# Attention and two MLPs on one core: one weight conversion less in the head's middle, and two groups of first products kept open there instead of three

## The chip, the cores and the metric

One of the eight cores of a Trainium2 chip runs the whole program. The metric is the device time of one execution in microseconds (us). The engines are PE (TensorE, matrix products), DVE (VectorE), ACT (ScalarE), POOL (GpSimd) and SP (SyncE, which only issues DMAs here; ACT issues some as well). Each engine works through its own instructions in the order of the program and meets the others only at semaphores.

## The reference, cut to what matters

```python
scores = scale * q @ k.T + min(bias, 0), causal          # 2 batches x 8 heads, 576 tokens, head size 64
x = softmax(scores) @ v                                  # 1152 tokens x 512
h = x @ w_in ; y = max(0.01 * h, h) @ w_out              # first MLP, 2048 hidden
out = sum_e p_e * (max(y @ w1[e], 0) @ w2[e])            # 4 experts, 1024 hidden, p_e from domain_probs
```

`w_in` and `w_out` come as 64-bit numbers and are converted on the chip to 32-bit ones, sixteen pieces of 128x1024.

## The kernel before, in words

Nearly every instruction is issued through a wrapper at line 43 that keeps program order on its engine, so the order on each engine is the order in which the Python code below calls it, and all rows name L43.

**Attention.** The work is cut into 16 units (a batch, a pair of heads, and either the first 256 or the last 320 tokens). A unit of the first kind has 4 items, one of the second kind 6. `attention()` walks over the items: step `i` issues the scores of item `i`, the exponentials of item `i-1`, the transposes of item `i-3`, the products with the values of item `i-5` and the finish of item `i-7`, and it yields three times a step, so that other work can be put in between. Scores go to `ps_sc`, DVE writes them with their row minimum to `z`, ACT takes the exponential, PE transposes to `ps_pt`, ACT copies to `pv`, PE multiplies with the values into `ps_o` (one buffer), DVE divides into `xo`, PE transposes that to `ps_x`, ACT and DVE write `x0` as a rounded part and a remainder.

**The weights.** `supply()` converts one piece in six calls: ACT takes the absolute value of the upper words into `raw`; then two `TENSOR_SCALAR` and two `SCALAR_TENSOR_TENSOR` on DVE, 128x1024 each; then `finished`, which is called after the next piece's ACT operation: it stores `raw` to DRAM (`w_f`), fetches a further 1 MB piece, and, where a buffer is free and no reload is under way, calls `split_w`:

```python
nc.scalar.copy(w[:, 0], raw)                                              # rounded part, on ACT
nc.gpsimd.tensor_tensor(w[:, 1], raw, f32(w[:, 0]), ALU.subtract)         # remainder, on POOL
```

Pieces that are not split at once are reloaded later from `w_f` by `late_splits()`. There are three `raw` buffers for conversions and reloads together. For the second kind of units POOL also forms the remainders `qs` and `ks`.

**The first products.** `opening()` computes the first 128-row tiles of `x @ w_in` while attention still runs: for each of four slices `kk` (one pair of heads) it adds three products of 512 columns to each open group `ps_u`, which is a PSUM bank of `ps_mm` (three banks in this phase, one of them first used by `nothing`). The second of the three products reads the remainder of the weights.

**The head** is the loop up to step 38, in which units 0 to 7 end. At the transposes of a step it puts products of zeros on PE (`idling(n)`, `n` products 128x128 into `nothing`, without use for the result) or one step of `opening`; at a step's end it calls `supply()` once in some steps. **The weave** is the second loop, steps 39 to 86: with the other 8 units it runs 82 steps of the first MLP and twice a step one call of `late_splits()` and `supply()`. Then the rest of the first MLP follows with nothing of attention beside it, then the second half of its tokens and the experts.

Of the kernel before, what the change touches and what calls it, by code (L numbers as in the profile page):

```python
# [9 lines left out]
F32 = mybir.dt.float32  # L10
# [9 lines left out]
def attention_moe_moe2(ctx: ExitStack, tc: tile.TileContext, q, k, v, s, w_in, w_out, probs, w1, w2, out):  # L20
# [34 lines left out]
    P = 128  # L55
    KD = DM // P
# [55 lines left out]
    def fetch64(n):  # L112
        src, (rows, _) = stream[n][:2]
        r64 = r64p.tile([P, 1024, 2], U32, tag="r64", name="r64")
        r64s.append(r64)
        nc.scalar.dma_start(r64.rearrange("p (a b) t -> p a (b t)", a=rows), src)
# [122 lines left out]
    def in_order(blocks):  # L239


        for i in range(len(blocks) + 1):
            if i < len(blocks):
                yield "up", blocks[i], 0
            if i > 0:
                yield "down", blocks[i - 1], None
            if i < len(blocks):
                yield "up", blocks[i], 1
# [5 lines left out]
    def fetch(n):  # L254

        if fixed:
            return
        for i in range(len(ready), min(n, len(stream))):
            if i not in raws:
                raws[i] = load_w(*stream[i][:3])  # L260
        for i in range(len(ready), min(n, len(stream))):
            ready.append(split_w(raws.pop(i), stream[i][1], stream[i][4]))
# [3 lines left out]
    def next_w(k):  # L266

        nonlocal used, retired
        retired = used
        used += k  # L270
        fetch(used + look)
        return ready[used - k : used]
# [7 lines left out]
    def in_steps(ps, pairs):  # L280

        for i, ((wh, wl), (xh, xl)) in enumerate(pairs):
            for j, (a, b) in enumerate(((wh, xh), (wl, xh), (wh, xl))):
                nc.tensor.matmul(ps, a, b, start=(i == j == 0), stop=(i == len(pairs) - 1 and j == 2))
            if i < len(pairs) - 1:
                yield

    def at(x, *where):
        return x[(slice(None), 0) + where], x[(slice(None), 1) + where]

    x_t, y_t, oacc, touched = [], {}, {}, {}
# [4 lines left out]
    def evict_up(ps, h):  # L296
        ht = hpool.tile([P, 2, sizes[0]], F32R, tag="h", name="ht")
        h.append(ht)
        hi, lo = at(ht)
        nc.scalar.activation(hi, ps, AF.Prelu, alpha=0.01)  # L300
        nc.scalar.activation(ps, ps, AF.Prelu, alpha=0.01)
        nc.vector.tensor_tensor(lo, ps, f32(hi), ALU.subtract)

    def up1(w, h, tiles=(0, 1)):

        for i in tiles:
            sl = slice(i * P, (i + 1) * P)
            ps = ps_mm.tile([P, 512], F32, tag="mm", name="ps_u")
            yield from in_steps(ps, [(at(w, kk, sl), at(x_t[0], kk)) for kk in range(KD)])
            evict_up(ps, h)  # L310
            yield

    def opening(h):

        w = next_w(2)
        ps = [ps_mm.tile([P, 512], F32, tag="mm", name="ps_u") for _ in range(3)]
        for kk in range(KD):
            for i in range(3):
                wi, sl = w[i // 2], slice(i % 2 * P, (i % 2 + 1) * P)
                for j, (l, m) in enumerate(((0, 0), (1, 0), (0, 1))):  # L320
                    nc.tensor.matmul(ps[i], wi[:, l, kk, sl], x_t[0][:, m, kk], start=(kk == j == 0), stop=(kk == KD - 1 and j == 2))
                if kk == KD - 1:
                    evict_up(ps[i], h)
                yield
        yield from up1(w[1], h, (1,))

    def down1(f, c, h, w):

        if f == 0:
            y_t[c] = ypool.tile([P, KD, sizes[c]], F32, tag=f"y{c}", name=f"y{c}")  # L330
        for d in (0, 2, 1, 3):
            for lo, hi in halves(c):
                ps = ps_mm.tile([P, 512], F32, tag="mm", name="ps_d")[:, : hi - lo]
                sl, cols = slice(d * P, (d + 1) * P), slice(lo, hi)
                at_h = [at(x, cols) for x in h] if c == 0 else [at(x, j, cols) for x in h for j in range(2)]
                yield from in_steps(ps, [(at(w[i // 2], i % 2, sl), x) for i, x in enumerate(at_h)])
                ya = y_t[c][:, d, cols]
                if f == 0:
                    nc.scalar.copy(ya, ps)
                else:  # L340
                    nc.vector.tensor_tensor(ya, ps, ya, ALU.add)
                yield
# [111 lines left out]
    def mlps(blocks):  # L454
        hs = {}
        for what, (e, f, c), pair in in_order(blocks):
            h = hs.setdefault(f, [])
            if what == "down":
                yield from down1(f, c, h, next_w(2))
            elif c == 0 and f == 0:  # L460
                if pair == 0:
                    yield from opening(h)
            elif c == 0:
                yield from up1(next_w(1)[0], h)
            else:
                h.append(paired_up(next_w(1)[0], c, True))
                yield
# [20 lines left out]
    ps_mm = banks.enter_context(tc.tile_pool(name="ps_mm", bufs=3, space=PSUM))  # L488
# [39 lines left out]
    def idling(n):  # L528

        for _ in range(n):  # L530
            nc.tensor.matmul(nothing[:, :P], idle, idle, start=True, stop=True)
# [174 lines left out]
    done = 0  # L706
# [33 lines left out]
    def hidden_pool(stack, n):  # L740
        nonlocal hpool
        hpool = stack.enter_context(tc.tile_pool(name="hpool", bufs=n))
# [5 lines left out]
    with ExitStack() as phase:  # L748
        x_t[0] = phase.enter_context(tc.tile_pool(name="x0pool", bufs=1)).tile([P, 2, KD, sizes[0]], F32R, name="x0")
        wpool = phase.enter_context(tc.tile_pool(name="wpool", bufs=4))  # L750
        r64p = phase.enter_context(tc.tile_pool(name="r64p", bufs=2))
        side, units_of_w, late, opened = attention(), supply(), late_splits(), 0
        nothing = ps_mm.tile([P, 512], F32, tag="mm", name="nothing")
        with tc.tile_pool(name="early", bufs=1) as early:
            ones = pads(early)
            cumulative()
            main = mlps(phases[0])

            for at_ in range(3 * 64):
                i = next(side)  # L760
                if done == 2 * NP:
                    break
                if at_ % 3 == 0 and i in (6, 8):
                    nc.scalar.copy(q_s[i // 2 - 3][D:DK, 1], ones[D:DK])
                if at_ % 3 == 1:
                    if i < 20:
                        idling(2)
                    elif i >= 22 and opened < 3 * (done // 2) and (opened < 6 or i >= 30):
                        next(main)
                        opened += 1  # L770
                if at_ % 3 == 2:
                    if i in (1, 5):
                        fetch64(i // 4)
                    if i >= 8 and (i < 21 or i >= 29):
                        next(units_of_w)
        hidden_pool(phase, 6)

        owed = 0
        for at_, i in enumerate(side):
            if at_ % 3 < 2:  # L780
                owed += WOVEN * KD / (2.0 * (48 - 6))
                while owed >= 1.0:
                    next(main)
                    owed -= 1.0
            if at_ % 3 != 1:
                next(late, None)
                next(units_of_w, None)
        attn.close()
        w7pool = ctx.enter_context(tc.tile_pool(name="w7pool", bufs=2, side="right"))
        scratch = ctx.enter_context(tc.tile_pool(name="scratch", bufs=2, side="right"))  # L790
        t7pool = ctx.enter_context(tc.tile_pool(name="t7pool", bufs=1, side="right"))
        tokens = paired_steps(1, x_t[1], t7pool)
        banks.close()
        ps_mm = ctx.enter_context(tc.tile_pool(name="ps_all", bufs=8, space=PSUM))

        sevens = first_sevens()
        for m, _ in enumerate(main):
            if m % 2 == 0:
                next(late, None)
            if m % 4 == 0:  # L800
                next(tokens, None)
            if m % 4 == 2:
                next(units_of_w, None)
            if m % 4 % 2 and m >= 4:
                next(sevens, None)
        for _ in sevens:
            pass
        for _ in tokens:
            pass
# [57 lines left out]
```

## Time and profile before

| | |
|---|---|
| time, median of 3 runs | 748.9 us (747.37 to 749.19) |
| the profiled execution's own time | 745.92 us |
| its span, first to last instruction | 744.1 us |
| busy: PE, DVE, ACT, POOL | 97%, 57%, 44%, 44% |
| mean granted clock of PE | 0.989 of full speed |
| chain that ended last, by engine | PE 83%, DVE 6%, ACT 4%, DMA 2%, issue 2%, POOL 1% |

A busy share is an average over stages with different limits, and pipelined matrix products make a PE that has little to do look busy. So the stages are read one by one, and in each the waits of PE.

### The profile page before, as it was taken

Reading aid. Unit: us, or ns where it says so; the run is one execution under the profiler, and the core shown is the slowest. Engines: PE = TensorE matmul, PEld = TensorE weight load, DVE = VectorE, ACT = ScalarE, POOL = GpSimd, SP = SyncE. Lnnn points to the kernel's source line nnn. Section 1 sums busy time; section 2 is a strip of 40 time slices with the busy share of each in tenths; the row PEclk is TensorE's granted clock in tenths of the full one; section 3 lists DMA queues with packets and bytes.
Section 4 is the critical chain, followed back from the end, with each engine's and each line's share of the span. In section 5 each row is a group of like instructions: output and inputs, shape, how many; then the busy total and the mean of one; then the engine's idle time right before and its main releaser. Section 6 shows DMA issues by size and latency. Waiting matters only on the chain.

```text
span 744.1 us, 11402 instructions
## 1 busy us (share of the span) xinstructions
PE 718.6 (97%) x4388; PEld 652.7 (88%) x4388; DVE 424.4 (57%) x850; ACT 330.7 (44%) x643; POOL 324.0 (44%) x250
## 2 busy tenths in 40 slices
PE   9998889999999999999999999999999999999997
PEld 8887668788887899999988988989889898898996
DVE  4856787589825755853784444644445444454452
ACT  5668676677663666553351232312313223142220
POOL 4134354343236978895255271542705427053200
PEclk9999899999999999999999999999999999999999
DMA  6785666865431223221021210201102012020002
GB/s 162 221 215 161 194 166 199 268 205 195 151 109 62 58 92 107 85 86 58 29 78 36 57 57 1 86 29 57 56 1 86 29 57 58 0 80 7 1 29 99
DMA packets 40890, 69.39 MB, mean 93 GB/s; under 512 B 4004, under 2 KB 22980, under 8 KB 40836
## 3 DMA queue, kind: packets, MB, share of 16 engines
q1 hardware_dynamic: 32132, 43.50, 20.0%
q10 hardware_dynamic: 8704, 25.17, 10.0%
q8 instruction: 34, 0.56, 0.3%
q14 instruction: 20, 0.16, 0.1%
HBM read 57.83 MB, written 10.82 MB: 92 GB/s over the span
## 4 chain that ended last, share of the span: by engine, by line
PE 83%; DVE 6%; ACT 4%; DMA 2%; issue 2%; POOL 1%; ACTq 0%; SPq 0%; DVEq 0%; POOLq 0%
PE ps_d L43 40%; PE ps_u L43 33%; PE ps_o L43 5%; DVE raw L43 3%; PE ps_sc L43 3%; PE ps_pt L43 2%; DMA qr<-in_q_dram 1%; DMA r<-in_moe_w_in_dram 1%; DVE z L43 1%; PE nothing L43 1%; ACT z L43 1%; DVE t L43 1%; ACT w L43 1%; ACT pv L43 1%; ACT ps_u L43 0%
## 5 line engine op out<-in xcount | busy, mean ns | idle before, releaser
L43 POOL TENSOR_TENSOR w<-raw,w 128x1024 fp32r<-128x1024 f32 (+2 forms) x88 | 148.3, 1700 | 316.3 <-ACT w L43 303.1
L43 PE MATMUL ps_u<-t,w 128*128 128x320 f32 (+1 forms) x1680 | 237.3, 299 | 2.2 <-DVE t L43 1.2
L43 PEld LDWEIGHTS ps_u<-t,w 128*128 128x128 f32 x1680 | 233.2, 189 | 6.3 <-ACT w L43 1.5
L43 PE MATMUL ps_d<-w,ht 128*128 128x512 f32 x864 | 203.3, 391 | 0.0
L43 PEld LDWEIGHTS ps_d<-w,ht 128*128 128x128 f32 x864 | 160.2, 188 | 31.9
L43 ACT ACTIVATE ht<-ps_u 128x320 fp32r<-128x320 f32 (+2 forms) x176 | 74.4, 433 | 162.1 <-DVE ps_u L43 132.3
L43 PE MATMUL ps_d<-ht,w 128*128 128x320 f32 (+1 forms) x576 | 110.8, 342 | 0.9 <-DVE y L43 0.9
L43 DVE SCALAR_TENSOR_TENSOR oacc<-ps_d,pn,oacc 128x512 f32<-128x512 f32 x63 | 47.3, 751 | 104.3 <-PE ps_d L43 104.3
L43 ACT CAST w<-raw 128x1024 fp32r<-128x1024 f32 (+2 forms) x88 | 64.0, 757 | 83.6 <-PE ps_d L43 70.5
L43 PEld LDWEIGHTS ps_d<-ht,w 128*128 128x128 f32 x576 | 91.5, 189 | 6.8 <-ACT t L43 1.3
L43 PEld LDWEIGHTS ps_o<-vs,pv 128*128 128x128 f32 x480 | 65.6, 197 | 15.2 <-issue 8.8
L43 PE MATMUL ps_o<-vs,pv 128*128 128x65 f32 x480 | 65.0, 273 | 8.3 <-issue 5.4
L43 DVE TENSOR_TENSOR ps_u<-ps_u,tmp 128x320 f32<-128x320 f32 (+1 forms) x120 | 56.4, 471 | 27.5 <-PE ps_u L43 26.1
L43 DVE SCALAR_TENSOR_TENSOR ht<-ps_u,ht 128x320 fp32r<-128x320 f32 (+1 forms) x128 | 56.3, 452 | 23.3 <-ACT ht L43 22.0
L43 POOL TENSOR_TENSOR w<-sums,w 128x1024 fp32r<-128x1024 f32 x24 | 58.7, 2444 | 6.1 <-ACT w L43 6.1
L43 DVE TENSOR_TENSOR tmp<-ps_u,tmp 128x320 f32<-128x320 f32 (+1 forms) x80 | 37.0, 464 | 42.2 <-PE ps_u L43 40.2
L43 PE MATMUL ps_u<-x,w 128*128 128x512 f32 x192 | 58.7, 422 | 0.0
L43 DVE CUSTOM_DVE_ANT_0 z<-ps_sc,mask 128x256 f32<-128x256 f32 (+4 forms) x80 | 40.8, 512 | 29.3 <-PE ps_sc L43 22.6
L43 ACT ACTIVATE z<-z,mn 128x256 f32<-128x256 f32 (+4 forms) x80 | 48.6, 607 | 13.2 <-DVE mn L43 11.3
L43 ACT COPY pv<-ps_pt 128x512 f32<-128x512 f32 (+3 forms) x96 | 38.8, 422 | 26.8 <-PE ps_pt L43 24.1
L43 PE MATMUL ps_pt<-ident,z 128*128 128x128 f32 x240 | 42.6, 286 | 7.3 <-ACT pv L43 7.3
L43 DVE TENSOR_TENSOR ht<-ps_u,ht 128x320 fp32r<-128x320 f32 (+1 forms) x48 | 26.5, 555 | 34.8 <-ACT ps_u L43 34.8
(72 smaller groups left out, 661.1 us busy)
## 6 DMA issues: line engine op xcount, KB each, us to landing
raw<-in_moe_w_dram SPq DMA_DIRECT2D x32, 512.0 KB
raw<-w_f SPq DMA_DIRECT2D x26, 512.0 KB
r<-in_moe_w_in_dram ACTq DMA_DIRECT2D x8, 1024.0 KB
w_f<-raw ACTq DMA_DIRECT2D x16, 512.0 KB
r<-in_moe_w_out_dram ACTq DMA_DIRECT2D x8, 1024.0 KB
qr<-in_q_dram SPq DMA_DIRECT2D x16, 160.0 KB
kr<-in_k_dram SPq DMA_DIRECT2D x8, 288.0 KB
vs<-in_v_dram SPq DMA_DIRECT2D x8, 256.0 KB
```

The costliest lines, as they stand in the source:

```text
L43: ins = call(*args, **kw)
```

## The change: what it does

In the loop of the head: zeros are issued two at a time up to step 7, then one at a time wherever no step of `opening` stands, up to step 37 (before: two at a time up to step 19). `opening` keeps two groups instead of three, needs one piece of weights instead of two, and its first step stands at step 16 instead of step 22; six of its steps are done by the end of the head instead of nine. `supply()` is called in steps 8 to 14 and from 29 on, instead of 8 to 20 and from 29 on. The rest of both follows later in the program.

```diff
     def opening(h):
 
-        w = next_w(2)
-        ps = [ps_mm.tile([P, 512], F32, tag="mm", name="ps_u") for _ in range(3)]
+        (w,) = next_w(1)
+        ps = [ps_mm.tile([P, 512], F32, tag="mm", name="ps_u") for _ in range(2)]
         for kk in range(KD):
-            for i in range(3):
-                wi, sl = w[i // 2], slice(i % 2 * P, (i % 2 + 1) * P)
+            for i in range(2):
                 for j, (l, m) in enumerate(((0, 0), (1, 0), (0, 1))):
-                    nc.tensor.matmul(ps[i], wi[:, l, kk, sl], x_t[0][:, m, kk], start=(kk == j == 0), stop=(kk == KD - 1 and j == 2))
+                    nc.tensor.matmul(ps[i], w[:, l, kk, i * P : (i + 1) * P], x_t[0][:, m, kk], start=(kk == j == 0), stop=(kk == KD - 1 and j == 2))
                 if kk == KD - 1:
                     evict_up(ps[i], h)
                 yield
-        yield from up1(w[1], h, (1,))
...
-            elif c == 0 and f == 0:
-                if pair == 0:
-                    yield from opening(h)
+            elif c == f == pair == 0:
+                yield from opening(h)
...
                 if at_ % 3 == 1:
-                    if i < 20:
-                        idling(2)
-                    elif i >= 22 and opened < 3 * (done // 2) and (opened < 6 or i >= 30):
+                    if i < 16:
+                        idling(2 if i < 8 else 1)
+                    elif opened < 2 * (done // 2) and (opened < 4 or i >= 30):
                         next(main)
                         opened += 1
+                    else:
+                        idling(1)
                 if at_ % 3 == 2:
                     if i in (1, 5):
                         fetch64(i // 4)
-                    if i >= 8 and (i < 21 or i >= 29):
+                    if 8 <= i < 15 or i >= 29:
                         next(units_of_w)
```

PE at steps 16 and 17, before: scores, transposes, two zeros, values.

```order
L43 MATMUL ps_sc<-ke_116,qe_115 128x256 [waits DMAHW6_49,DMAHW7_49,DMAHW0_49,DVE_49]
L43 MATMUL ps_pt<-ident,z 128x128 [waits DVE_49]
L43 MATMUL ps_pt<-ident,z 128x128
L43 MATMUL nothing<-idle 128x128 x2
L43 MATMUL ps_o<-vs,pv 128x65
```

The same place of the change, with the next step:

```order
L43 MATMUL ps_sc<-ke_116,qe_115 128x256 [waits DMAHW6_49,DMAHW7_49,DMAHW0_49,DVE_49]
L43 MATMUL ps_pt<-ident,z 128x128 [waits DVE_49]
L43 MATMUL ps_pt<-ident,z 128x128
L43 MATMUL ps_u<-x_102,w 128x512 [waits Activation_49]
L43 MATMUL ps_u<-x_102,w 128x512 [waits Pool_49]
L43 MATMUL ps_u<-x_102,w 128x512
L43 MATMUL ps_o<-vs,pv 128x65
L43 MATMUL ps_sc<-ke_116,qe_115 128x256 [waits DVE_49]
L43 MATMUL ps_pt<-ident,z 128x128 [waits Activation_49]
L43 MATMUL ps_u<-x_102,w 128x512 x3
L43 MATMUL ps_o<-vs,pv 128x65 [waits DMAHW5_49,DVE_49,PE_49]
```

The zeros have made room for the first two steps of `opening`, and the second product of the first of them waits for POOL's remainder of the weights.

POOL in the weave, before: `w` is the remainder of a split piece; `qs` and `ks` come as a pair, one pair for each unit of the second kind. The rows go from the split ahead of the fourth pair to the one behind the fifth.

```order
L43 TENSOR_TENSOR w<-raw,w 128x1024
L43 TENSOR_TENSOR qs<-qr,qs 64x640
L43 TENSOR_TENSOR w<-raw,w 128x1024
L43 TENSOR_TENSOR ks<-kr,ks 64x1152
L43 TENSOR_TENSOR w<-raw,w 128x1024
L43 TENSOR_TENSOR qs<-qr,qs 64x640
L43 TENSOR_TENSOR ks<-kr,ks 64x1152
L43 TENSOR_TENSOR w<-raw,w 128x1024
```

The same stretch of the change:

```order
L43 TENSOR_TENSOR w<-raw,w 128x1024
L43 TENSOR_TENSOR qs<-qr,qs 64x640
L43 TENSOR_TENSOR w<-raw,w 128x1024
L43 TENSOR_TENSOR ks<-kr,ks 64x1152
L43 TENSOR_TENSOR w<-raw,w 128x1024
L43 TENSOR_TENSOR qs<-qr,qs 64x640
L43 TENSOR_TENSOR w<-raw,w 128x1024
L43 TENSOR_TENSOR ks<-kr,ks 64x1152
L43 TENSOR_TENSOR qs<-qr,qs 64x640
```

The fifth pair, and further on the seventh, now have a `w` between their two operations, and the sixth no longer has one ahead of it. In the head one of two splits ahead of the first pair is gone, so each `w` here is the piece before. The split ahead of the fourth pair came out of `late_splits()` before, with a reload; now it stands right behind its conversion, one step earlier in the program.

## Rows read from the trace of the kernel before

**Rows 1.** Busy time by stage: engines, granted clock, DMA share, GB/s.
```profile
28.48:37.14 8.66, 7.92 (x60) 6.92 (x59) 7.89 (x25) 6.19 (x16) 2.35 (x1) 1.00 0.94 289
37.14:68.97 31.83, 28.11 (x180) 24.05 (x180) 19.80 (x63) 23.59 (x51) 13.46 (x6) 0.95 0.81 212
68.97:220.60 151.63, 139.91 (x874) 122.59 (x873) 110.65 (x195) 107.23 (x176) 55.29 (x23) 0.95 0.56 181
```

**Rows 2.** Timeline of PE, steps 14 to 16: start, duration, instruction.
```profile
27.20 0.39 PE L43 MATMUL ps_x<-ident,xo 128*128 128x128 f32 x2
...
28.48 0.65 PE L43 MATMUL ps_sc<-ke,qe 128*128 128x256 f32 x2
...
29.19 0.61 PE L43 MATMUL nothing<-idle 128*128 128x128 f32 x4
29.64 0.33 PE L43 MATMUL ps_o<-vs,pv 128*128 128x65 f32 x2
```

**Rows 3.** Timeline of ACT at the end of step 14.
```profile
27.62 0.37 ACT L43 CAST x<-ps_x 128x256 fp32r<-128x256 f32 x1
27.63 0.35 ACTq L43 DMA_DIRECT2D w_f<-raw  x1
28.02 1.05 ACT L43 CAST w<-raw 128x1024 fp32r<-128x1024 f32 x1
```

**Rows 4.** Timeline of POOL, the head's first split.
```profile
29.21 2.35 POOL L43 TENSOR_TENSOR w<-raw,w 128x1024 fp32r<-128x1024 f32 x1 [19.71 <-ACT w L43]
```

**Rows 5.** Timeline of PE: a wait for DVE, and the scores of step 22.
```profile
35.53 0.70 PE L43 MATMUL ps_sc<-ke,qe 128*128 128x256 f32 x2 [0.33 <-DVE mn L43]
...
37.14 0.44 PE L43 MATMUL ps_sc<-ke,qe 128*128 128x128 f32 x2
```

**Rows 6.** Timeline of DVE, one operation of a conversion at step 17.
```profile
30.76 1.36 DVE L43 TENSOR_SCALAR raw<-raw 128x1024 uint32<-128x1024 uint32 x1
```

**Rows 7.** Timeline of PE, the first step of the opening at step 22.
```profile
37.44 0.94 PE L43 MATMUL ps_u<-x,w 128*128 128x512 f32 x3
38.22 0.56 PE L43 MATMUL ps_o<-vs,pv 128*128 128x65 f32 x4
```

**Rows 8.** Timeline of PE: long waits in the head's end and the weave.
```profile
62.33 1.33 PE L43 MATMUL ps_pt<-ident,z 128*128 128x128 f32 x5 [1.84 <-ACT pv L43]
...
112.23 1.30 PE L43 MATMUL ps_o<-vs,pv 128*128 128x65 f32 x10 [3.34 <-issue]
...
145.82 0.33 PE L43 MATMUL ps_pt<-ident,z 128*128 128x128 f32 x1 [0.75 <-ACT pv L43]
...
149.91 0.77 PE L43 MATMUL ps_pt<-ident,z 128*128 128x128 f32 x5 [2.03 <-ACT pv L43]
...
175.75 1.30 PE L43 MATMUL ps_o<-vs,pv 128*128 128x65 f32 x10 [0.99 <-DVE xo L43]
```

**Rows 9.** Busy time in stretches of 4 us, columns as in group 1.
```profile
60.00:64.00 4.00, 2.15 (x11) 1.83 (x11) 1.21 (x5) 4.00 (x7) 3.66 (x2) 0.78 1.02 316
64.00:68.00 4.00, 4.00 (x27) 3.56 (x28) 3.91 (x8) 2.47 (x6) 1.65 (x1) 0.79 0.91 238
...
172.00:176.00 4.00, 3.01 (x20) 2.39 (x19) 3.93 (x11) 4.00 (x7) 0.20 (x1) 1.00 0.11 43
```

**Rows 10.** Timeline of POOL around the fourth pair and before the sixth.
```profile
98.14 3.02 POOL L43 TENSOR_TENSOR w<-raw,w 128x1024 fp32r<-128x1024 f32 x1 [16.32 <-ACT w L43]
...
103.09 2.38 POOL L43 TENSOR_TENSOR w<-raw,w 128x1024 fp32r<-128x1024 f32 x1
...
140.56 2.39 POOL L43 TENSOR_TENSOR w<-raw,w 128x1024 fp32r<-128x1024 f32 x1 [10.29 <-DMA vs<-in_v_dram]
```

**Rows 11.** Timeline of DVE beside the fourth pair.
```profile
99.47 2.24 DVE L43 TENSOR_SCALAR raw<-raw 128x1024 f32<-128x1024 f32 x1
...
102.24 3.78 DVE L43 TENSOR_SCALAR raw<-raw 128x1024 uint32<-128x1024 uint32 x1
```

**Rows 12.** Timeline of ACT before the sixth pair.
```profile
142.99 1.12 ACT L43 ACTIVATE raw<-r 128x1024 f32<-128x1024 f32 x1 [2.56 <-POOL w L43]
```

## The prediction, made before the changed kernel ran

> **What bounds the kernel now.** I read the page's busy shares first (PE 97%), then the busy time by stage [rows 1], then the timeline of PE stage by stage for the waits that a share hides. The reader is to see that PE is what everything waits for, and that it loses time in three ways. In steps 16 to 21 the conversion keeps DVE busy for 7.89 of 8.66 us, and PE waits for it a little in each step [rows 1, 5, 6]. At the end of the head and in the weave PE has long waits, of 1.84, 3.34 and 2.03 us, for ACT or DVE [rows 8]. And behind such a wait it runs at the lower of its two clock levels for a while: around the wait of 1.84 us the granted clock is 0.78 and 0.79 in two stretches of 4 us, while behind the wait of 0.99 us it stays 1.00 [rows 8, 9]. A granted clock of 0.78 means that (1 - 0.78) / 0.5 = 44% of the stretch went at 1.2 GHz; both stretches make 3.4 us of it, and where PE is the limit half of that is lost, **1.7 us** (a dip, below).
>
> The program has the same products of weights before and after, and one product of zeros more (0.22 us, half the 0.45 us from the two zeros to the next instruction [rows 2]). Three steps of the opening leave the head; there one takes 0.78 us of PE [rows 7], and behind the weave, where nothing stands beside it, about as much. So all that counts is what PE loses: which waits go, which come.
>
> **The change, part by part.**
>
> *The conversion that leaves the head's middle.* Steps 16 to 21, from the scores of step 16 to those of step 22, take 8.66 us [rows 2, 5], in which PE is busy for 7.92 [rows 1]. The 0.74 us left over are the least that it loses there to DVE; as overlapping products look longer than they are, it is more, at most the 1.8 us of the eight zeros that stand there only to fill time. The loss goes with the DVE operations (four a conversion, one of them 1.36 us long [rows 6]): I take **-1.0**, nearer the busy time that was read. What ACT and POOL no longer do there hides behind PE. The store and the 1 MB fetch that go with it load the DMA engines less (0.94 busy there [rows 1]); I take no gain from that, it may be 0.5 us.
>
> *The opening at step 16, and the weights that it reads.* This is the new wait. The call that splits the first piece still stands at the end of step 14; only the reader has moved, from step 22 to step 16. Its chain: from the `ps_x` products of step 14 (27.20) over ACT's `x` and the issue of the store to the rounded part (28.02 plus 1.05), and POOL's remainder, 29.21 plus 2.35 = 31.56 [rows 2 to 4]. That is 4.36 us behind `ps_x`, with some 0.1 for the signal 4.45. PE reaches the place where the zeros of step 16 stood 1.99 us behind `ps_x` [rows 2], 0.22 sooner with one zero less at step 15; the first product needs only the rounded part and takes 0.26 (a third of 0.78 [rows 7]); so the second is reached after 2.0 us and waits **2.4 us**. The bounds are 2.1 and 2.8. It does not depend on when all this happens, as both ways start at the same `ps_x`; that PE gets there faster by its zeros makes the wait longer, not the start of POOL earlier. Queued behind the waiting product on PE are the values of step 16 and the scores of step 17, so DVE, ACT and the whole pipeline of items wait too. The conversion's work on DVE could have used the pause, but it has just been taken out.
>
> *The clock behind that wait.* Waits of 1.84 us and more were followed by a dip, one of 0.99 us was not [rows 8, 9]. 2.4 us lies among the former: **+1.7**, between 0 (what PE did before was dense) and 3.4 (two such stretches).
>
> *Fewer zeros, spread further.* From step 8 to 15 eight zeros go, worth 1.8 us where PE has nothing else to wait for, and about as many stand at steps 18 to 37: as work they cancel. But a zero also filled the time in which the next unit's first values wait for `xo`; with one instead of two PE has 0.22 us less cover, in each of some four units, of which I take **+0.5** in waits (0 to 0.9). Those in steps 36 to 38 stand where PE works without a pause behind the wait of 1.84 us, and do not fill that wait, as they are queued behind the transposes that wait. The extra zero: **+0.2**.
>
> *The weave.* The calls of the conversion come six later, which is one whole conversion, so each kind of DVE operation stays beside the same kind of attention step; what changes is which splits POOL does beside them. Where POOL works, DVE's operations get long, and each ends the same time after POOL's: the one of 30.76 ends 0.56 us after POOL's first split [rows 4, 6], those of 99.47 and 102.24 (2.24 and 3.78 us) 0.55 us after the splits of 98.14 and 103.09 [rows 10, 11]. It looks as if each had waited and then taken some 0.55 us. DVE then comes to `xo` late, and PE waits 3.34 us [rows 8]. The Trainium skill, SBUF — State Buffer, "Who interferes with whom", says that DVE's two-port operations and those with two SBUF inputs share a port pair with GpSimd under an exclusive lock. By that rule a split set between two other operations of POOL stops DVE for its whole length, which speaks against this change; these three rows agree with it. Gains: the split ahead of the fourth pair now stands a step earlier, where PE waits anyway, so DVE's 2.24 us may shrink to 0.55; of these 1.7 I take -1.1, as POOL's other three operations there stay. The split ahead of the sixth pair goes; it held ACT for 2.56 us [rows 12], and PE's two waits of 0.75 and 2.03 us [rows 8] came of that: -2.8, and half a dip, -0.8. Losses: the fifth and seventh pair get a split in their middle, 2.38 us each by the rows [rows 10], less 0.4 us of slack: +2.0 each (0 where DVE slips in between, 3.34 plus a dip, 5.0, where it goes as at the fourth pair). Net **-0.7**.
>
> Sum: -1.0 + 2.4 + 1.7 + 0.5 + 0.2 - 0.7 = **+3.1 us**. The profiled execution took 745.92 us (its span is 744.1), so 749.0 for its like; the median of the runs shown is 748.9, 3.0 above it, and what is forecast is a median: **752.0 us**.
>
> **The rivals.**
>
> *A: the wait comes, the dip does not.* +3.1 - 1.7 = +1.4, 750.3 us. For it: the wait of 2.03 us with a dip behind it had another of 0.75 ahead of it [rows 8], and at step 16 PE comes from dense work. Against: the dip behind 1.84 us [rows 8, 9]. Within 0.3% (2.25 us, about what a measurement here can tell from no change).
>
> *B: no wait, since the opening's remainder is there in time.* Then the change does in the head what it is laid out to do: +3.1 - 2.4 - 1.7 = -1.0, 747.9 us. For it would be a POOL that starts sooner; against it, POOL has been idle for 19.71 us when it starts [rows 4], so nothing on POOL can be taken out of its way.
>
> *C, the other side: POOL's order frees the weave.* The 3.34 us at the fourth pair fall below 1 us, and its dip goes (-2.35 - 1.7 in place of -1.1); the waits at the sixth pair go with their whole dip (-4.5 in place of -3.6); and the two new splits, with POOL ahead of its work, cost 0.5 each in place of 2.0. That is -3.0 - 0.9 - 3.0 = -6.9 against the forecast: 745.1 us. It decides where `xo` at the fourth pair comes 2.35 us sooner. For it: the split that went is as long as that. Against: POOL's three further operations there stay.
>
> *D: the lock rules.* If both new splits act as the fourth pair does, each costs 5.0 in place of 2.0: +6.0, 758.0 us. For it: the order at the fifth pair is now row for row that of the fourth. Against: from the wait at 112.23 to the one at 145.82 PE had none [rows 8], so there is some slack to eat first.
>
> **How the numbers follow.** Forecast 0.42, A 0.16, B 0.08, C 0.20, D 0.14. The forecast's own bounds (some 2.5 us either way) put 0.30 of its 0.42 beyond +2.25 us, 0.11 within and 0.01 on the other side. Slower: 0.30 + 0.14 of D + 0.05 of A = 0.49. Same: 0.11 + 0.11 of A + 0.05 of B + 0.04 of C = 0.31. Faster: 0.16 of C + 0.03 of B + 0.01 = 0.20. C's terms reach below 744 and D's above 760; the range 745.5 to 757.5 leaves about a tenth out at each end.
>
> **What would show it.** In the timeline of PE at step 16 the second product of `ps_u` has a wait for POOL's `w` of 2.1 to 2.8 us, and the granted clock of the next 4 us is under 0.9. In the 9 us before step 22 DVE has no 128x1024 operation. The scores of step 39 start at about 70.5 (68.97 now [rows 1], plus the head's terms of 3.8, less three steps of the opening, 2.3). No ACT row waits over 2 us for POOL's `w` before the sixth pair. PE has a new wait for `xo` in the fifth pair's unit. The prediction is wrong if the second product does not wait, if the wait is made good before the head ends (because ACT or DVE, not PE, paces steps 22 to 38), or if the weave's waits move by more than 3 us.

## The result, and the profile after

| | before | after |
|---|---|---|
| time, median (range) | 749.22 us of 6 executions (747.37 to 750.67) | 755.73 us of 6 (754.04 to 759.4) |
| ratio, 95% interval | | 1.0098 [1.0074, 1.0122] |
| the profiled execution's span | 744.1 us | 752.5 us |
| its mean granted clock | 0.989 | 0.982 |

The changed kernel is slower by 7.3 us by the ratio (0.0098 of 749). Medians here and below are of all executions; the ratios, each against the kernel before on the same chip, leave out three of e4's ten executions (757.67 to 761.36 us, clock 0.968 to 0.972) and one of e7's twelve (876.06 us, clock 0.749). So 3.1 us was forecast and more than twice that came. The spans of the two profiled executions differ by 8.4 us, a little more, as the one of the kernel before (745.92 us) is faster than all six of its kernel in the table.

The first view is the busy time of two stretches, the head with the first steps of the weave (to 78 us) and the weave (columns as in [rows 1]). The kernel before:

```profile
0.00:78.00 78.00, 70.82 (x488) 63.35 (x489) 47.32 (x149) 54.58 (x116) 27.07 (x35) 0.98 0.71 195
78.00:220.00 142.00, 130.53 (x813) 114.46 (x813) 105.92 (x185) 98.64 (x162) 51.52 (x22) 0.95 0.57 184
```

The changed kernel:

```profile
0.00:78.00 78.00, 69.40 (x448) 62.30 (x449) 43.28 (x142) 47.84 (x106) 21.48 (x32) 0.91 0.56 158
78.00:220.00 142.00, 127.78 (x796) 112.22 (x794) 115.02 (x188) 99.27 (x163) 51.92 (x22) 0.95 0.59 187
```

PE is idle for 22.8 us of the 220 (220 less 69.40 and 127.78), before for 18.7. What the clock takes is a stretch's length times one less its granted clock, since half of the time spent at 1.2 GHz is lost: 78 x 0.09 + 142 x 0.05 = 14.1 us, before 8.7. Together that is 9.5 us more, against 8.4 in the span; clocks are read to a hundredth, and idle time at the low clock is counted twice. In these two executions about four parts in ten of the loss are waits and six are clock. The clock's part lies in the first stretch alone (0.91 against 0.98; 0.95 in the second, before and after), and whether it belongs to the change or to the execution that was profiled has to be seen.

**Step 16**, the timeline of PE:

```profile
28.48 0.51 PE L43 MATMUL ps_u<-x,w 128*128 128x512 f32 x1
30.98 0.72 PE L43 MATMUL ps_u<-x,w 128*128 128x512 f32 x2 [2.00 <-POOL w L43]
```

POOL's row that it waits for, which answers to [rows 4], and the clock of the 8 us around it:

```profile
28.57 2.36 POOL L43 TENSOR_TENSOR w<-raw,w 128x1024 fp32r<-128x1024 f32 x1 [19.08 <-ACT w L43]
```

```profile
28.00:32.00 4.00, 2.00 (x11) 1.42 (x11) 0.55 (x5) 1.96 (x6) 2.36 (x1) 1.00 1.00 309
32.00:36.00 4.00, 4.00 (x32) 3.69 (x31) 1.95 (x10) 2.02 (x7) 0.00 (x0) 1.00 0.56 174
```

The wait stands where it was forecast and for what was forecast. The clock stays at 2.4 GHz behind it.

**The end of the head**, where [rows 8] had the 1.84 us: PE's two waits for ACT, and the granted clock (before the last two columns).

```profile
62.10 0.77 PE L43 MATMUL ps_pt<-ident,z 128*128 128x128 f32 x5 [1.64 <-ACT pv L43]
...
64.40 1.11 PE L43 MATMUL ps_pt<-ident,z 128*128 128x128 f32 x4 [0.56 <-ACT pv L43]
```

```profile
62.00:64.00 2.00, 1.75 (x11) 1.25 (x11) 0.64 (x3) 2.00 (x5) 1.92 (x2) 0.83 1.00 366
64.00:66.00 2.00, 1.60 (x8) 1.60 (x9) 2.00 (x3) 1.42 (x4) 1.42 (x1) 0.50 0.97 267
...
74.00:76.00 2.00, 2.00 (x8) 1.71 (x8) 1.81 (x5) 0.54 (x2) 0.00 (x0) 0.50 0.00 0
76.00:78.00 2.00, 2.00 (x12) 1.87 (x12) 0.82 (x2) 2.00 (x4) 0.00 (x0) 0.76 0.03 8
```

The first wait is a little shorter than before (1.64 us against 1.84), the second, of 0.56 us, is new; PE then runs at 1.2 GHz for 13.6 us (0.7 in the first row, 12.0 in the six rows of 0.50 that begin and end with the second and the third, 1.0 in the last), where before it was 3.4. That this long stretch comes from the change is not shown: e7 and e11 (below) have the head of the kernel before, unchanged, and in the 20 us from 60 to 80 their clocks are 0.66 and 0.74, as low as the changed kernel's 0.66, where the profile of the kernel before has 0.91. First e7, then e11:

```profile
60.00:80.00 20.00, 17.47 (x84) 15.54 (x84) 11.99 (x28) 13.20 (x24) 6.22 (x4) 0.66 0.44 126
60.00:80.00 20.00, 17.45 (x91) 15.92 (x92) 10.09 (x23) 13.73 (x26) 6.79 (x4) 0.74 0.51 150
```

In e7 the low time there is 13.6 us as well, behind waits of 1.85 and 0.67 us.

**The weave**: the values of each unit's first item, which wait for the `xo` of the unit before.

```profile
91.28 1.94 PE L43 MATMUL ps_o<-vs,pv 128*128 128x65 f32 x8 [3.10 <-issue]
114.89 0.88 PE L43 MATMUL ps_o<-vs,pv 128*128 128x65 f32 x3 [2.35 <-issue]
138.70 0.52 PE L43 MATMUL ps_o<-vs,pv 128*128 128x65 f32 x3 [1.71 <-issue]
159.51 0.74 PE L43 MATMUL ps_o<-vs,pv 128*128 128x65 f32 x5 [2.48 <-issue]
180.01 1.19 PE L43 MATMUL ps_o<-vs,pv 128*128 128x65 f32 x9 [2.02 <-issue]
200.86 1.30 PE L43 MATMUL ps_o<-vs,pv 128*128 128x65 f32 x10 [2.49 <-issue]
```

Every one starts 0.66 us behind the start of an `xo` on DVE (the fourth at 158.85, below), which is why they are read as waits for DVE though the releaser shown is "issue". They come once a unit, beside the third to the eighth pair, and add up to 14.15 us. Before, PE's waits of over 0.5 us beside these pairs came to 10.33: those of [rows 8] from 112.23 on and two beside the third pair.

```profile
79.81 0.77 PE L43 MATMUL ps_pt<-ident,z 128*128 128x128 f32 x5 [1.11 <-ACT pv L43]
...
86.23 2.36 PE L43 MATMUL ps_o<-vs,pv 128*128 128x65 f32 x10 [2.11 <-issue]
```

What stands ahead of `xo` is shown by DVE and POOL beside the third and the sixth pair. POOL:

```profile
83.99 3.00 POOL L43 TENSOR_TENSOR ks<-kr,ks 64x1152 fp32r<-64x1152 f32 x1
...
153.11 2.71 POOL L43 TENSOR_TENSOR w<-raw,w 128x1024 fp32r<-128x1024 f32 x1
...
186.76 2.38 POOL L43 TENSOR_TENSOR w<-raw,w 128x1024 fp32r<-128x1024 f32 x1 [10.45 <-ACT w L43]
```

DVE at the same places, and beside the eighth pair:

```profile
84.50 3.57 DVE L43 SCALAR_TENSOR_TENSOR raw<-r,raw 128x1024 uint32<-128x1024 uint32 x1
...
88.47 1.21 DVE L43 SCALAR_TENSOR_TENSOR raw<-r,raw 128x1024 uint32<-128x1024 uint32 x1
...
153.62 3.29 DVE L43 SCALAR_TENSOR_TENSOR raw<-r,raw 128x1024 uint32<-128x1024 uint32 x1
...
158.85 0.56 DVE L43 TENSOR_TENSOR xo<-ps_o,st 128x384 f32<-128x384 f32 x1
...
187.36 2.87 DVE L43 SCALAR_TENSOR_TENSOR raw<-r,raw 128x1024 uint32<-128x1024 uint32 x1
...
199.19 0.68 DVE L43 TENSOR_TENSOR y<-ps_d,y 128x512 f32<-128x512 f32 x1
```

A `SCALAR_TENSOR_TENSOR` of 128x1024 takes 1.21 us where POOL is idle (88.47); the three long ones end 1.08, 1.09 and 1.09 us after POOL's operation does. It looks as if they did nearly all their work after POOL had finished.

### The profile page after: what moved, and what is told of

Same layout as the page of the kernel before. It is cut to its first block, busy times and chain, and to the rows that moved or that the text cites. A ratio compares the mean times of both kernels' runs of the same rounds, so it can differ in the third digit from the quotient of the medians.

```text
span 752.5 us, 11403 instructions
## 1 busy us (share of the span) xinstructions
PE 722.8 (96%) x4390; PEld 657.6 (87%) x4390; DVE 431.1 (57%) x850; ACT 331.1 (44%) x643; POOL 323.2 (43%) x250
## 4 chain that ended last, share of the span: by engine, by line
PE 92%; DVE 3%; issue 3%; POOL 1%; ACT 1%; POOLq 0%; ACTq 0%; DVEq 0%
PE ps_d L43 40%; PE ps_u L43 35%; PE ps_o L43 7%; PE ps_sc L43 5%; PE ps_pt L43 4%; PE nothing L43 1%; DVE raw L43 1%; DVE t L43 1%; PE ps_x L43 1%; POOL qe L43 0%; POOL w L43 0%; DVE z L43 0%; DVE ht L43 0%; ACT z L43 0%; DVE ps_u L43 0%
## 5 line engine op out<-in xcount | busy, mean ns | idle before, releaser
L43 PEld LDWEIGHTS ps_o<-vs,pv 128*128 128x128 f32 x480 | 67.8, 205 | 23.6 <-issue 17.9
L43 PE MATMUL ps_o<-vs,pv 128*128 128x65 f32 x480 | 68.0, 281 | 16.5 <-issue 14.8
L43 DVE SCALAR_TENSOR_TENSOR raw<-r,raw 128x1024 uint32<-128x1024 uint32 x32 | 50.3, 1572 | 0.3
```

The lines of the kernel that those rows point to most:

```text
L43: ins = call(*args, **kw)
```

## The experiments

Two theories. *Waits*: PE's waits, at step 16 and for `xo` in the weave, are the loss, and the low clock follows them. *Clock*: the loss is a longer stretch at 1.2 GHz at one place, the end of the head. Behind them stands the question which part of the change makes it.

### Parts of the change undone

Opening at step 18 (a line of `idling` in each of steps 16 and 17 in its place) and at step 22:

```diff
-                    if i < 16:
+                    if i < 18:                      # e1_open18;  i < 22: e8_open22
```

> The changed kernel with the first step of the opening at step 18 instead of 16 (a single product of zeros in steps 16 and 17). Theory 1 (the wait for POOL at step 16 is lost PE time): the wait of 2.0 us shrinks to under 0.3 us, step 34 comes about 2 us sooner and the kernel takes 753 to 754 us instead of 755.7. Theory 2 (what counts is the long stretch at 1.2 GHz at the head's end, since ACT and DVE pace the steps from 30 on): the 2 us are taken back by longer waits for ACT and DVE before step 36, the stretch at 1.2 GHz stays near 13 us, and the time stays within 1 us of 755.7.

> The changed kernel with the opening's first step at step 22, where it stood before, and one product of zeros in each of steps 16 to 21; two groups and the one conversion less in the head's middle stay. The wait for POOL's remainder cannot come. By the prediction's sum the wait and its dip (4.1 us) go: 751 to 752. By the rival that the loss lies in the head's end and the weave, where two groups and the later conversions put other splits beside the same steps: 754 to 757, with PE's waits in the weave those of the changed kernel.

The conversion back in the head's middle, and no zeros from step 33 on:

```diff
-                    if 8 <= i < 15 or i >= 29:
+                    if 8 <= i < 21 or i >= 29:      # e2_conv_back
-                    else:
+                    elif i < 33:                    # e3_no_late_zeros
```

> The changed kernel with the second conversion back in the head's middle (calls in steps 8 to 20 as before); two groups, the opening at step 16 and the zeros stay as changed. Theory 1 (the splits that moved in POOL's order make new waits in the weave): POOL's order in the weave is that of before again, the waits near 139, 181 and 201 us go, the waits of before come back, and the kernel takes 751 to 753 us. Theory 2 (the low clock at the head's end is the cost): the stretch at 1.2 GHz behind step 35 stays over 10 us and the time stays at 755 or goes up by the 1 us that DVE then costs in steps 16 to 21.

> The changed kernel without the products of zeros in steps 33 to 38 (six fewer). Theory 2a (the zeros at the head's end are in PE's way and stretch the low-clock part): unit 7 ends 1 to 4 us sooner and the kernel takes 752 to 754.5 us. Theory 2b (the zeros there are what little keeps PE busy): the stretch at 1.2 GHz does not get shorter, and the time is 755 to 758 us. Theory 1 says nothing of it but the six zeros' own 0.7 us at most where PE is the limit: 755 us.

The kernel before, with two groups alone (`opening` as in the change, from step 22, zeros and conversion as before):

> The kernel before with one part of the change alone: two groups in the opening instead of three (first step at step 22 as before, six steps in the head instead of nine, conversions and zeros as before). Theory 1: POOL's order in the weave stays that of before, so at most 1 us either way: 748.5 to 750.5 us. A rival (the three steps that leave the head are lost, since the head has idle PE time to put them in): they cost their 2.1 us behind the weave, 751 to 752 us.

| | ratio to before |
|---|---|
| the change | 1.0098 [1.0074, 1.0122] |
| e1, opening at 18 | 1.0074 [1.0031, 1.0117] |
| e8, opening at 22 | 1.0043 [1.0014, 1.0073] |
| e2, conversion back | 1.0108 [1.0068, 1.0149] |
| e3, no late zeros | 1.0128 [1.0104, 1.0153] |
| e4, before with two groups alone | 1.0025 [0.9995, 1.0055] |

With the opening at step 22 there is no wait for POOL, and 0.0055 of the time comes back, 4.1 us (with some 2.9 either way from the two intervals). The other 3.2 us stay, so the early opening is not the whole loss. Step 18 lies between and is told from neither: its profiled execution has no wait at the opening and only 3.4 us at 1.2 GHz in the head's end, but a clock of 0.90 from 78 to 220 us, and its span, 752.2 us, is that of the changed kernel. The late zeros cost nothing that can be measured.

The conversion in the head's middle makes no difference in time that can be measured here, and the theory that it makes the weave's waits by moving POOL's order fails: with it back in its place (e2) neither the order from the sixth pair on nor the waits of before came back. PE beside the fifth, sixth and eighth pair of e2, with 3.07, 2.34 and 2.01 us beside the third, fourth and seventh:

```profile
137.76 1.30 PE L43 MATMUL ps_o<-vs,pv 128*128 128x65 f32 x10 [0.79 <-issue]
...
160.25 2.37 PE L43 MATMUL ps_o<-vs,pv 128*128 128x65 f32 x10 [4.16 <-issue]
...
206.97 1.30 PE L43 MATMUL ps_o<-vs,pv 128*128 128x65 f32 x10 [2.52 <-issue]
```

In e4, which has two groups and nothing else of the change, PE waits 2.92, 2.35, 4.17, 2.00 and 1.42 us at the same places, none at the fifth. POOL's order there has the split in the middle of the seventh pair, none ahead of the sixth, and not yet the split in the middle of the fifth. So the waits of the weave come in the main with the two groups; the likely way is that the weave's products start three steps behind. With the conversion comes the fifth pair's, about 0.9 us of it (1.71 against 0.79). In time, two groups alone are slower by 1.9 us by the ratio, an interval that just includes no change; the median of all ten executions is 753.57 us, 4.4 above the kernel before, and the rival of that expectation (751 to 752) fits as well.

The stretches of e8 show where its loss lies (its profiled span is 7.8 us above the one of the kernel before, more than the 3.2 of the ratio):

```profile
0.00:78.00 78.00, 70.44 (x499) 63.09 (x499) 48.92 (x149) 55.59 (x118) 27.30 (x35) 1.00 0.65 182
78.00:220.00 142.00, 125.39 (x749) 110.19 (x748) 111.75 (x183) 92.22 (x151) 45.27 (x20) 0.92 0.55 176
```

Its head is no worse than before, with a clock of 1.00 to 78 us and unit 7 done at 66.09 us (68.83 before; three steps of the opening, 2.3 us, have left it), and its weave is worse: PE idle for 16.6 us there (11.5 before), the clock 0.92 (0.95). PE's wait at step 36 is 1.64 us here too, with no low clock behind it. The head's end alone, as the theory of the clock has it, is thus not the place.

### The wait at the head's end filled

```diff
+                if at_ % 3 == 0 and i in (36, 37):
+                    idling(6 if i == 36 else 2)
```

> The changed kernel with six more products of zeros ahead of the transposes of step 36 and two ahead of those of step 37, where PE waited 1.64 and 0.56 us for ACT's pv and then ran 13.6 us at a low clock; nothing else differs, so the zeros stand in time that was lost. Theory of the clock (most of what the change costs is a longer stretch at 1.2 GHz behind that wait): PE's wait there falls below 0.5 us, the stretch goes or shrinks to some 3.5 us, unit 7 ends 3 to 6 us sooner, and the kernel takes 750 to 752. Theory of the waits (what counts is the sum of PE's waits, the clock follows the execution and not the place): as the changed kernel, 755 to 757, the low stretch coming elsewhere.

Measured 751.3 us (747.7 to 756.93), ratio 1.0033 [1.0002, 1.0064]. PE at step 36 with the six zeros (two rows each), and the clock:

```profile
63.25 1.50 PE L43 MATMUL nothing<-idle 128*128 128x128 f32 x12
64.59 0.71 PE L43 MATMUL ps_pt<-ident,z 128*128 128x128 f32 x5
```

```profile
64.00:68.00 4.00, 3.93 (x35) 3.75 (x34) 2.22 (x6) 3.82 (x8) 3.69 (x2) 1.00 0.82 270
68.00:72.00 4.00, 4.00 (x35) 3.76 (x34) 3.13 (x9) 1.91 (x4) 0.00 (x0) 1.00 0.67 175
```

The wait and the low clock behind it are gone, and 0.0065 of the time came back, 4.9 us (again some 2.9 either way), as the theory of the clock had it, for work that computes nothing. The same zeros in the kernel before, whose head can have the same low stretch, were not tried. But the profiled execution, at 755.88 us one of the slowest, has a clock of 0.96 to 78 us (a low stretch behind the wait at step 16 and another ahead of the zeros), and 0.92 in the weave. So the low clock has more than one place.

### The waits of the weave filled with products

Three steps of the MLP more ahead of the first values of each unit, fewer in the next step, in the changed kernel (e6) and in the kernel before (e7):

```diff
                 owed += WOVEN * KD / (2.0 * (48 - 6))
+                if at_ % 3 == 1 and i % 6 == 1:
+                    for _ in range(3):
+                        next(main)
+                        owed -= 1.0
```

> The changed kernel with the steps of the MLP in the weave placed otherwise: three more of them ahead of the first values of each unit, where PE waits for xo, and as many fewer in the next step. Seven waits of 1.7 to 3.1 us are to be filled with real work, some 1.5 us each. Theory of the waits: 8 to 12 us less, 744 to 748, as work that stood behind attention now stands in the waits. Theory that DVE or ACT paces the weave (each unit takes as long as DVE needs for its items and conversions): the waits move to the next step and the time stays within 2 us of the changed kernel's, 754 to 758.

> The kernel before with the same placing of the MLP's steps in the weave. Theory of the waits: its waits of 1.1, 2.1, 3.3 and 1.0 us are filled for the most part, 3 to 5 us less, 744 to 746, so that the distance to the changed kernel with this placing shrinks to 0 to 3 us. Theory that DVE or ACT paces the weave: 748 to 751, and the distance stays at 6.

e6: 741.09 us (737.68 to 745.19), ratio 0.9892 [0.9861, 0.9923]. e7: median 742.59 us (eleven of the twelve from 739.28 to 747.47), ratio 0.9922 [0.9891, 0.9952]. PE at the third pair of e6, the nine products ahead of the first values:

```profile
82.59 2.33 PE L43 MATMUL ps_u<-x,w 128*128 128x512 f32 x9
86.64 1.30 PE L43 MATMUL ps_o<-vs,pv 128*128 128x65 f32 x10 [1.71 <-issue]
```

The 3.10 us are 1.71; the others became 0.73, 0.65, 1.10, 0.82 and 0.20. That took 2.0% off the changed kernel and 0.8% off the one before, and the two no longer differ measurably. The theory of the waits holds so far: the weave's waits are time that other work can use, and the changed kernel has more of it. The clock of the profiled execution is 0.98 in both stretches, but the first placed steps stand at 82.59 us, so that the low stretch in the head is not away because of them. How the 7.3 us divide stays open: the 4.1 of e8, the 4.9 of e5 and the 9.6 by which e6 gains more than e7 (2.06% and 0.78% of 749) are 18.6 together, so the gains do not add.

### What makes xo late

DVE's own queue: the conversion's second `SCALAR_TENSOR_TENSOR`, 1.2 us, moved from ahead of `xo` to behind it.

```diff
-                next(units_of_w, None)
+                for _ in range(1 if i % 6 else at_ % 3):
+                    next(units_of_w, None)
```

> The changed kernel with one call of the conversion moved in every sixth step of the weave: the SCALAR_TENSOR_TENSOR of 1.2 us that stands on DVE right ahead of the operations that end in xo comes right behind them; nothing else differs. Theory that DVE's queue ahead of xo makes PE's waits for the first values: each of the six waits of 1.7 to 3.1 us falls by 1.2 us, 6 to 8 us less in all with what the low clock gives back, 747 to 750. Theory that POOL's splits pace it (the operation ahead of the moved one ends only after POOL, and the rest is hidden): waits as before the move, 753 to 757.

POOL: the keys' remainder cut short from the third pair on (the edit also gives `ks` buffers of its own, not shown).

```diff
-        nc.gpsimd.tensor_tensor(ks[D:], kr, f32(ks[:D]), ALU.subtract)
+        kc = slice(0, S if n < 2 * NP + 2 else D)
+        nc.gpsimd.tensor_tensor(ks[D:, :, kc], kr[:, :, kc], f32(ks[:D, :, kc]), ALU.subtract)
```

> The changed kernel in which POOL, from the third pair on, forms the remainder of the keys for 64 columns of each head only (the rest keeps old numbers, so the scores are not the reference's), in buffers of its own kind; its 2.6 to 3.0 us become some 0.3. Theory of the lock (DVE's long operations end 0.55 us or a little more after POOL's): the 3.57 and 3.29 us operations ahead of xo fall to 1.2, PE's waits of 3.1, 1.7 and 2.5 us to about 1, and the kernel to 745 to 750. Theory that DVE's own queue is too long whatever POOL does: waits within 0.5 us of the changed kernel's, 753 to 757.

e9: 745.86 us (743.66 to 748.62), ratio 0.9963 [0.9946, 0.9981]. DVE at the third pair:

```profile
83.18 3.58 DVE L43 SCALAR_TENSOR_TENSOR raw<-r,raw 128x1024 uint32<-128x1024 uint32 x1
...
88.18 0.56 DVE L43 TENSOR_TENSOR xo<-ps_o,st 128x384 f32<-128x384 f32 x1
88.65 1.22 DVE L43 SCALAR_TENSOR_TENSOR raw<-r,raw 128x1024 uint32<-128x1024 uint32 x1
```

The waits fell by 1.1 to 1.2 us at the third, fourth, fifth and eighth pair (to 1.96, 1.18, 0.58 and 1.36), by 2.5 at the sixth, where one of 0.81 us for the next scores came, and by 1.0 at the seventh. The order of one operation is worth 1.3% of the kernel; 747 to 750 us were expected.

e12: 732.54 us (732.29 to 733.39), ratio 0.9782 [0.9757, 0.9807]. POOL and DVE at the third pair:

```profile
78.77 0.79 POOL L43 TENSOR_TENSOR ks<-kr,ks 64x128 fp32r<-64x128 f32 x1
```

```profile
79.28 1.36 DVE L43 SCALAR_TENSOR_TENSOR raw<-r,raw 128x1024 uint32<-128x1024 uint32 x1
```

The operation of 3.57 us takes 1.36 and again ends 1.08 after POOL's. The largest wait left at a unit's first values is 0.97 us. Six remainders of the keys, 17.0 us of POOL's time, became 3.7; the span is 21.7 us shorter. PE's idle time to 220 us gives 8.4 of it (14.4 in place of 22.8), and the clock, now 1.00 in both stretches, the 14.1 us of above: a little more than all. Half of these 14.1 us, the 7.0 of the head, is not shown to come from the edit, as the first shortened remainder stands at 78.77 us, behind the head; yet the mean clock of all five executions is 0.997 or more, of the changed kernel's six 0.977 to 0.984, and why is not known. In the weave alone the waits give 8.6 us and the clock 7.1. The expectation, 745 to 750, was far too careful: it counted the waits and not the clock. Both theories of `xo` have a part in the truth, the queue on DVE and POOL's hold on it; the two edits were not run together. The same cut in the kernel before was not tried, so how much of this is the change's and how much was there already stays open.

### All together

e10 is the changed kernel with the edits of e5, e6, e8 and e9; e11 is the kernel before with those of e6 and e9.

> The changed kernel with all that helped so far and the moved call: the opening at step 22, zeros in the two waits of steps 36 and 37, three more steps of the MLP ahead of the first values of each unit in the weave, and the conversion's call behind xo. If the losses are PE's waits in the weave and the low clock behind them, they are nearly gone: 734 to 739, under the 741.1 of the placing alone. If the move only shifts the wait to the next scores (DVE is as busy in all): 740 to 743.

> The kernel before with the placing of the MLP's steps and the moved call. Its DVE queue ahead of xo holds the same 1.2 us operation, but its waits are fewer after the placing (two, of 0.73 and 1.34 us), so the move has less to take: 740 to 743 (742.6 without it). If it falls as far as the changed kernel with both, the two kernels differ by nothing but where their waits lie.

e10: 738.55 us (736.71 to 741.36), ratio 0.9863 [0.9836, 0.9891]: a version 1.4% faster than the kernel before and 2.3% faster than the changed one. e11: 742.01 us (737.44 to 744.78), ratio 0.9895 [0.9862, 0.9928]. Beyond the placing alone e10 gained 0.3%, inside the intervals: what e5, e8 and e9 gave by themselves does not come on top of it. A part of the wait moved on to the next scores:

```profile
88.15 0.48 PE L43 MATMUL ps_sc<-ks,qs 128*128 128x448 f32 x1 [2.27 <-DVE mn L43]
```

DVE there stood behind the eviction of the group that the three steps had just closed:

```profile
86.02 0.69 DVE L43 TENSOR_TENSOR ht<-ps_u,ht 128x512 fp32r<-128x512 f32 x1 [2.49 <-ACT ps_u L43]
```

## Why the prediction came out as it did

The direction and the first cause were right, and the measured time lies in the range; the sum of 3.1 us was too small by 4.2. That the range held is in part luck: the forecast's own bounds, 2.5 us either way, end at 754.5, and it is D that stretches the range to 757.5. By the prediction's own sign (the weave's waits move by more than 3 us; they moved by 3.8) the account behind the sum was wrong. The step that failed is the weave.

*The wait at step 16*: 2.00 us for POOL's `w`, forecast 2.4 (2.1 to 2.8). POOL's end came 4.36 us behind `ps_x` (26.57 to 30.93), as forecast. What was mis-sized is PE's arrival: the first product came 1.91 us behind `ps_x` and took 0.51 us, not 0.26, so that the second was reached 2.4 us behind `ps_x` and not 2.0. That wait and its dip were put at 2.4 + 1.7 = 4.1 us; e8 against the change measures 4.1, with 2.9 either way, so that the wait alone would fit as well.

*The dip behind it* did not come in the profiled execution (clock 1.00 from 28 to 36 us). In that of e5 the same wait, 1.99 us, was followed by one: 0.86 over the 12 us from 28 to 40, 1.7 us lost. Of the seven profiled executions with this wait, e2, e3, e5 and e9 have 0.86 there, the change, e6 and e12 have 1.00. The size of the dip was right; whether it comes differs from one profiled execution to the next.

*The conversion* of the head's middle did leave: DVE is busy for 2.50 us of the 8 from 28 to 36. Its -1.0 and the zeros' +0.7 are below what the runs can resolve; e2 and e3 give no sign against them, and none for them.

*Step 39's scores* start at 72.55 us, forecast 70.5. Of the low stretch at the end of the head 9.2 us lie ahead of them, in place of 3.4, worth 2.9; against it stand the dip that did not come (1.7) and the shorter wait (0.4). The 1.2 us left over were not traced. The prediction had no term for a longer low stretch, and as the head of the kernel before has one of 13.6 us in e7, none is shown to belong to the change.

*The weave* was put at -0.7 us, on the ground that the later conversions change which splits POOL does beside which step. That ground failed: the waits of the weave come with the two groups (e2 and e4), and the prediction let the three steps of the opening leave the head as if only their 0.78 us each were moved. With the opening out of it (e8) the prediction's sum is -1.0 (conversion) + 0.7 (zeros) - 0.7 (weave) = -1.0 us; measured were +3.2, with 2.2 either way, and PE's idle time in the weave is 5.1 us more than before. In the change itself the waits beside the pairs grew by 3.8 us, where the terms of the sum make +0.1. By pair, in PE's waits of the profiled executions:

| pair | before | forecast change | after |
|---|---|---|---|
| third | 1.11 and 2.11 | 0 | 3.10 |
| fourth | 3.34 | -1.1 | 2.35 |
| fifth | none | +2.0 | 1.71 |
| sixth | 0.75 and 2.03 | -2.8 | 2.48 |
| seventh | 0.99 | +2.0 | 2.02 |
| eighth | none | 0 | 2.49 |

The fourth and the fifth came as worked out, the seventh at half. At the sixth the split ahead of the pair went, and with it ACT's wait of 2.56 us [rows 12] and PE's two waits; but the split right behind the pair (153.11) now held the conversion's operation for 3.29 us, and `xo` came 2.5 us late. The prediction followed the wait that went and did not ask what is late next. At the eighth nothing was forecast: the split now stands 4.3 us ahead of the pair (186.76 and 191.03; 175.80 and 184.96 before), held DVE's operation at 187.36 for 2.87 us, and the eviction of a product group (`y`, 0.68 us) now comes right ahead of `xo`, where before it came right behind it; the likely reason is that the weave's products are three steps behind. The prediction read POOL's order to the seventh pair and DVE's evictions not at all.

Of the rivals, D (758.0, the lock rules) was nearest, in the number (2.3 us off, the forecast 3.7) and in part in the mechanism: a split of POOL does stop DVE for what is left of its length. But D's own two places did not cost what it says: the wait is 1.71 us at the fifth pair and 1.0 us longer at the seventh, and the larger growth came at the eighth, which D does not have. The Trainium skill, SBUF — State Buffer, "Who interferes with whom", has an exclusive lock on a port pair that DVE shares with GpSimd; this case's rows agree with it, 3.57 us beside POOL's full remainder and 1.36 beside a short one. A's condition, the wait without the dip, held in the profiled execution, but its 750.3 did not come. B is out, as the wait came; C, that POOL's order frees the weave, is out as well: the waits there grew by 3.8 us.

## What to carry to other kernels

When an edit shifts one stream of work against another, follow every operation in the queue ahead of the result that the bound engine waits for (here what DVE and POOL do ahead of `xo`), for each repetition, and not only the rows that the edit names. Work that is only moved to a later stage (here three steps of products) shifts the streams of that stage as well. A wait that recurs once a unit can be filled from a stream that is free to move: three steps of products placed there were worth more (2.0%) than the whole change cost (1.0%). Count the clock with the waits: in the weave of e12 taking the waits away gave back 8.6 us, and the clock 7.1 more. And compare more than one profiled execution before a low stretch is put down to an edit: the same head showed 13.6 us of it and 3.4.

## What the runs showed of the hardware

**The same wait, another clock.** PE's wait for ACT at step 36 is 1.64 us in the changed kernel, 1.64 in e1 and 1.62 in e12. Behind it PE ran at 1.2 GHz for 13.6 us in the first, 3.4 in the second and not at all in the third. The head of the kernel before did the same: 3.4 us behind a wait of 1.84 us, 13.6 behind one of 1.85 in e7. The rows of the third, e12:

```profile
62.20 0.77 PE L43 MATMUL ps_pt<-ident,z 128*128 128x128 f32 x5 [1.62 <-ACT pv L43]
...
64.51 0.66 PE L43 MATMUL ps_pt<-ident,z 128*128 128x128 f32 x4 [0.74 <-ACT pv L43]
```

```profile
60.00:64.00 4.00, 2.15 (x16) 1.50 (x14) 1.70 (x7) 4.00 (x8) 3.79 (x2) 1.00 1.01 311
64.00:68.00 4.00, 3.49 (x30) 3.42 (x31) 4.00 (x6) 2.70 (x6) 1.52 (x1) 1.00 0.98 250
```

Executions of one kernel differ along with their clock: those of the kernel before that ran beside e5 to e8 go from 742.69 us at a mean clock of 0.995 to 753.7 at 0.981, those of e12, which has few waits left, from 732.29 to 733.39. One profiled execution shows which waits there are, not how long the clock stays low behind one. What decides between no low stretch and one of 13.6 us was not found.

**DVE behind POOL.** A 128x1024 operation of these kinds that meets POOL's on the way ended a fixed time after it, whatever its start: 0.55 us for the `TENSOR_SCALAR` [rows 10, 11], which takes 0.68 by itself, 1.08 to 1.09 for the `SCALAR_TENSOR_TENSOR` of 1.21. It looks as if nearly the whole operation runs after POOL's end, so what a POOL operation costs DVE is nearly all that is left of POOL's length when DVE comes to it. It goes the other way too: POOL's split at 157.62, which starts 0.32 us into an operation of DVE, takes 3.11 us and not 2.38.
